# Decode attention and MLP on one core: the K and V tiles move from SyncE's DMA queue to GpSimd's software queue

## The chip, the cores and the metric

The kernel runs on one core of one Trainium2 chip. The metric is the device time of one execution in microseconds; for the kernel before it is 1303.65 us, the median of three runs (1303.53 to 1303.67). Profiles show one execution, from its first to its last instruction (the span). PE is TensorE, DVE VectorE, ACT ScalarE, POOL GpSimd and SP SyncE; SPq and POOLq are the sequencers of those two engines as they issue DMAs.

## The reference

One token for each of two sequences goes through an attention block with a cache of 8192 keys and values in 32 heads, then through a channel MLP. All is float32.

```python
# x (2,1,512)  k_cache, v_cache (2,32,8192,128)  wq (512,4096)  wo (4096,512)  w1 (512,1792)  w2 (1792,512)
q = (layernorm(x) @ wq).reshape(B, 1, 32, 128).transpose(0, 2, 1, 3)
p = softmax(einsum("bhqd,bhkd->bhqk", q, k_cache) * 128 ** -0.5)
o = einsum("bhqk,bhkd->bhqd", p, v_cache).transpose(0, 2, 1, 3).reshape(B, 1, 4096)
h = x + o @ wo
# the MLP block has a layernorm of its own, behind the outer one
out = h + gelu(layernorm(layernorm(h)) @ w1 + b1) @ w2 + b2
```

The two caches are 537 MB of the 561 MB that the kernel reads; each element of them is used once.

## The kernel before

The work is cut into 32 units. A unit is a pair of heads of one sequence: `units = [(g, b) ...]`, with g from 0 to 15 and b from 0 to 1, so even units have b = 0 and odd units b = 1. A unit has a K tile and a V tile, each of 128 partitions by 16384 float32 (64 KB a partition, 8 MB in all). All large tiles share a ring of three slots (`slot()`, the tile `kv`): wq takes the first, then K0, K1, V0, K2, V1, K3, V2 and so on, and a load waits until what stood in its slot has been read.

For each unit, `multiply` (L464, VectorE) multiplies a quarter of the K tile, a chunk of 32 keys a partition, by q in place. `halve` (L468, GpSimd) adds the upper 64 products of each key to the lower 64, for the first three chunks of the four. `add_up` (L471, VectorE) sums what is left to the scores. The loop over chunks c issues multiply(c), halve(c) and then add_up(c - 1), and add_up(3) comes after the loop. `row_max` (L478) and, at odd units, `all_max` and `exps` make the softmax weights of a pair (TensorE, VectorE, ScalarE). `values` (TensorE, L241 in the loop over rounds) multiplies the weights with a V tile: that of an even unit at the end of the odd unit after it, that of an odd unit at c == 2 of the even unit after it. So V(i - 2) has been read by the time that unit i is well under way, and K(i) by the end of unit i. At five places `stage` (L418) copies the next three pairs' q on VectorE, at c == 1 of odd units.

All loads of K and V come from one helper, `load` (L438), that issues on SyncE's hardware queue; `load_wo` (L444) loads most of wo into a slot and gathers the rest with two indirect DMAs on GpSimd (L448); `load_last` (L456) loads the tile `wlast`. SyncE does nothing else, so a load that waits for its slot holds up only the loads behind it. In the unit loop the loads of a unit are issued ahead of its computation, in this order: wo (last unit only), V(i - 1), K(i + 1), wlast (unit 30 only). After the loop come the last V tile in four parts, the bias, w1 and w2 (L667 to L675), on SyncE.

Engines take their instructions in program order. Semaphores and waits are put in by the class `Waits`, from what each instruction reads and writes; DMAs signal on 12 semaphores in turn, with separate sets for SyncE or ScalarE and for GpSimd. The program is built with `dynamic_dma_scratch_size=1024`, the space for descriptors of the software queue.

Of the kernel before, what the change touches and what calls it, by code (L numbers as in the profile page):

```python
# [22 lines left out]
GH = 3  # L23
SR = 4
LW = 4
LEFT = (((0, 3), (5, 19), (20, 30), (44, 47), (55, 56), (64, 66), (68, 94), (103, 105), (108, 109), (119, 121)),
        ((0, 2), (5, 11), (12, 30), (44, 47), (56, 57), (64, 66), (68, 95), (103, 104), (108, 109), (112, 113),
         (119, 121)))
# [2 lines left out]
def kept(left):  # L31
    at, runs, n = 0, [], 0
    for a, b in (*left, (P, P)):
        if a > at:
            runs.append((at, n, a - at))
            n += a - at
        at = b
    return runs, n
# [234 lines left out]
def tile_decode_block(nc, waits, x, k, v, wq, wo, wog, wol, w1, bias, w2, out):  # L273
    B, H, SK, DH = k.shape
    D = wq.shape[0]
    F = w1.shape[1]
    DC = D // P
# [3 lines left out]
    NS2 = SK // HP  # L281
    ROW = NS2 * DH
# [3 lines left out]
    NU = len(units)  # L286
# [10 lines left out]
    def slot():  # L297
        return kv.tile([P, ROW], F32, name="kv", tag="kv")
# [3 lines left out]
    junk = const.tile([P, 3], F32, name="junk")  # L302
# [1 line left out]
    x2 = const.tile([B, D], F32, name="x2")  # L304
    nc.scalar.dma_start(x2, x)
    wqt = slot()
    nc.sync.dma_start(wqt, wq.rearrange("(p r) n -> p (r n)", r=DC))
    wqs = wqt.rearrange("p (r n) -> p r n", r=DC)

    wlast = wts.tile([P, LW, D], F32, name="wlast")  # L310
    ident = const.tile([P, P], F32, name="ident")
# [7 lines left out]
    oall = const.tile([P, 2, 2 * GP, B], F32, name="oall")  # L319
    NQ = len(LEFT)  # L320
    og = const.tile([P, NQ * SR + LW - TH, B], F32, name="og")
    slots = [kept(x) for x in LEFT]
    first_slot = [sum(n for _, n in slots[:q]) for q in range(len(LEFT))]
    HG = H - LW
    NS = (HG - 4 * GP) * DH // SR
# [4 lines left out]
    pms = {}  # L330
    for x in LEFT:
        if x not in pms:
            pms[x] = const.tile([P, P], F32, name=f"pm{len(pms)}")
            nc.gpsimd.memset(pms[x], 0.0)
            for p0, s0, n in kept(x)[0]:
                nc.gpsimd.tensor_copy(pms[x][:, p0:p0 + n], ident[:, s0:s0 + n])
    pm = [pms[x] for x in LEFT]
    FAR = 4096.0
    ioff = const.tile([P, len(LEFT)], F32, name="ioff")
    for q in range(len(LEFT)):  # L340
# [89 lines left out]
    for _ in range(SPARE):  # L430
        pe.matmul(rowacc[:, :B], wz, wz, start=True, stop=True)

    def load(src, i, parts):
        g, b = units[i]
        t = slot()
        rows = src[b, 2 * g:2 * g + 2].rearrange("h (p j) d -> (h p) (j d)", j=NS2)
        for s0, n in parts:
            nc.sync.dma_start(t[:, s0 * DH:(s0 + n) * DH], rows[:, s0 * DH:(s0 + n) * DH])  # L438
        return t

    def load_wo():
        t = slot()
        n = 2 * GP * D
        nc.sync.dma_start(t[:, :2 * n], wo)  # L444
        tv = t[:, :2 * n].rearrange("p (j c) -> p j c", j=2)
        gv = t[:, 2 * n:].rearrange("p (q r n) -> p q r n", q=len(LEFT), n=D)
        for q in range(len(LEFT)):
            nc.gpsimd.indirect_dma_start(  # L448
                out=gv[:, q].rearrange("p r n -> p (r n)"), out_offset=None,
                in_=wog,  # L450
                in_offset=bass.IndirectOffsetOnAxis(ap=gidx[:, q:q + 1], axis=0),
                bounds_check=NS - 1, oob_is_err=False)
        return tv.rearrange("p j (r n) -> p j r n", n=D), gv

    def load_last():
        nc.sync.dma_start(wlast.rearrange("p r n -> p (r n)"), wol)  # L456

    def chunk(t, c):
        return t[:, c * CH * DH:(c + 1) * CH * DH].rearrange("p (j d) -> p j d", d=DH)

    def multiply(i, c, t):
        g, b = units[i]
        kc = chunk(t, c)
        nc.vector.tensor_tensor(kc, kc, QP[g][:, b, None, :].to_broadcast([P, CH, DH]), op=ALU.mult)  # L464

    def halve(c, t):
        kc = chunk(t, c)
        nc.gpsimd.tensor_tensor(kc[:, :, 0:HP], kc[:, :, 0:HP], kc[:, :, HP:DH], op=ALU.add)  # L468
# [36 lines left out]
    def inverse(g):  # L505
        r = work.tile(list(RL[g].shape), F32, name="rl" if g < GL else "rlp")
        nc.vector.reciprocal(r, RL[g])  # L507
        RL[g] = r

    def by_head(g):  # L510
        r = RL[g]
        RL[g] = work.tile([4, 2], F32, name="rl2")
        nc.vector.tensor_scalar(RL[g], hmask, r, None, op0=ALU.mult)
# [23 lines left out]
    def head_out(g):  # L537
        op, rl = OP.pop(g), RL.pop(g)
        if g < GL:
            nc.vector.tensor_tensor(orow[:, g % GH], op[:, None, :].to_broadcast([4, 2, DH]),  # L540
                                    rl[:, :, None].to_broadcast([4, 2, DH]), op=ALU.mult)
            return
        nc.vector.tensor_tensor(otz[:, :, 0:32:16], *(x.rearrange("p (b s) -> p s b", b=B) for x in (op, rl)),
                                op=ALU.mult)

    def turn(j):
        rows = orow.rearrange("m k e d -> m (k e d)")
        if j < 4:
            TP[j] = psm.tile([HP, 2 * GP, 2 * B], F32, name="sm")
            rows = rows.rearrange("m (p r) -> m r p", r=2 * GP)  # L550
            for r in range(2 * GP):
                pe.transpose(TP[j][:, r, :], rows[:, r, :], ident[:4, :4])
            psm.turn("sm", 2)
            return
        TP[j] = psm.tile([P, NQ * SR + LW - TH, 2 * B], F32, name="sm")
        at, n = (HG - 4 * GP) * DH, LW - TH
        last = rows[:, at:at + n * DH].rearrange("m (p r) -> m r p", r=n)
        for r in range(n):
            pe.transpose(TP[j][:, NQ * SR + r, :], last[:, r, :], ident[:4, :4])
        rows = rows.rearrange("m (s r) -> m r s", r=SR)  # L560
        for q, (_, n) in enumerate(slots):
            s0 = first_slot[q]
            for r in range(SR):
                pe.transpose(TP[j][:n, q * SR + r, :], rows[:, r, s0:s0 + n], ident[:4, :4])
# [21 lines left out]
    def project_all(wot, wgt):  # L586
        so = so2[0]
        parts = [(oall[:, j, r, :], wot[:, j, r, :]) for j in range(2) for r in range(2 * GP)]
        parts += [(og[:, q * SR + r, :], wgt[:, q, r, :]) for q in range(NQ) for r in range(SR)]
        parts += [(og[:, NQ * SR + h, :], wlast[:, h, :]) for h in range(LW - TH)]  # L590
        n = len(parts)
# [6 lines left out]

    full = [(0, NS2)]
    assert NS2 == NCH * CH  # L600
    KT, VT = {0: load(k, 0, [(0, NS2 // 2), (NS2 // 2, NS2 // 2)])}, {}
    for i, (g, b) in enumerate(units):
        if i == NU - 1:
            wot, wgt = load_wo()
        if i >= 1:
            VT[i - 1] = load(v, i - 1, full)
        if i + 1 < NU:
            KT[i + 1] = load(k, i + 1, full)
        if i == NU - 2:
            load_last()  # L610
        kt = KT.pop(i)
        S[i] = work.tile([P, NS2], F32, name="s", bufs=3)
        for c in range(NCH):
            multiply(i, c, kt)
            if c < NCH - 1:
                halve(c, kt)
            if c == 0:
                if b == 0 and g >= 1:
                    inverse(g - 1)
                if b == 1 and g >= 1:  # L620
                    head_out(g - 1)
                elif b == 1:
                    nc.vector.memset(orow, 0.0)
                if i == NU - 1:
                    turn(4)
            elif c == 1:
                if b == 0 and g >= 1:
                    by_head(g - 1)
                if b == 0 and g % GH == 1:
                    turned(max(g // GH - 1, 0))  # L630
                if i == NU - 1:
                    turned(4)
                if b == 1 and g < GL:
                    make_q(g + 1)
                    if g % GH == GH - 1:
                        stage((g + 1) // GH)
            if c >= 1:
                add_up(i, c - 1, kt, HP)
            if c == 2 and b == 0 and i >= 1:
                values(i - 1, VT.pop(i - 1))  # L640
                gather(g - 1)
                head_sum(g - 1)
                if g == GL:
                    pe.end()
            if c == 2 and i == NU - 1:
                placed()
                project_all(wot, wgt)
        add_up(i, NCH - 1, kt, DH)
        if b == 0 and g % GH == 0 and g < GL:
            pe.round()  # L650
        row_max(i)
        if i == NU - 1:
            row_sum()
        if b == 1:
            all_max(g)
            exps(g)
            values(i - 1, VT.pop(i - 1))
            total(g)
            if g % GH == 0 and g < GL:
                turn(max(g // GH - 1, 0))  # L660

    vlast = load(v, NU - 1, [(0, NS2 // 2), (NS2 // 2, 32), (NS2 // 2 + 32, 24), (NS2 - 8, 8)])
    wt = slot()
    br = wt[:, 2 * DC * F:2 * DC * F + FN + P]
    b1r, b2r = br[:, :FN], br[:, FN:]
# [167 lines left out]
```

## Time and profile before

| | |
|---|---|
| device time, median of 3 | 1303.65 us |
| span of the profiled execution | 1302.4 us |
| bytes moved by DMA, mean rate | 561.20 MB, 431 GB/s |
| VectorE busy | 951.3 us (73%) |
| GpSimd busy | 442.5 us (34%) |
| TensorE matmul busy | 386.7 us (30%) |
| the 96 halvings on GpSimd | 433.4 us |
| packets of the hardware queue q1 | 11114 |
| packets of the software queue q0 | 288 |

The page lists no device time for the profiled execution beside its span; the median of the runs lies 1.25 us above that span. The page's first part gives busy time by engine, its second cuts the span into 40 slices with a digit for the busy tenths, its third lists the DMA queues (q0 is GpSimd's software queue, q1 SyncE's hardware queue, q8 and q14 fetch instructions), the fourth follows the chain of work that ended last back from the end, and the fifth groups instructions: busy time and mean, then the idle time of the engine before them and what ended it. The timeline shows start, duration, engine, line, operation and tiles in order of time.

### The profile page before, as it was taken

The numbers are of one execution on the slowest core, as the hardware profiler recorded it, in microseconds if no ns is written. First come the engines' busy times: TensorE is split into PE (matmuls) and PEld (weight loads), VectorE is DVE, ScalarE is ACT, GpSimd is POOL, SyncE is SP. The second block draws the span as 40 slices with busy tenths as digits, with TensorE's granted clock in tenths as the row PEclk, the third lists the DMA queues.
The fourth block names the chain that finished last, engine by engine and source line by source line (L and its number), as shares of the span: only waits on it lengthen the run. The fifth ranks groups of instructions, "written<-read, shape, count | busy, mean of one in ns | idle before, by whom it ended". The sixth has DMA issues, their size and how long they took to land.

```text
span 1302.4 us, 6774 instructions
## 1 busy us (share of the span) xinstructions
PE 386.7 (30%) x2900; PEld 122.8 (9%) x2900; DVE 951.3 (73%) x411; ACT 51.7 (4%) x172; POOL 442.5 (34%) x138
## 2 busy tenths in 40 slices
PE   3105033330413314033230413323032331403358
PEld 1101000000100001010000101000010100100113
DVE  1988677779777778777778877777976777877752
ACT  0010000000000000000000000000000000000011
POOL 1444422244432234432234442224442224443320
PEclk9556566575666657566665666667566665756669
DMA  9999999999999999999999999999999999999998
GB/s 403 435 449 418 445 423 443 425 435 433 429 439 431 439 431 435 427 443 423 443 427 439 431 431 439 431 437 429 439 427 441 425 439 431 431 439 429 432 426 370
DMA packets 11420, 561.20 MB, mean 431 GB/s; under 512 B 1404, under 2 KB 1412, under 8 KB 1806
## 3 DMA queue, kind: packets, MB, share of 16 engines
q1 hardware_dynamic: 11114, 559.97, 99.5%
q0 software_dynamic: 288, 1.05, 0.2%
q8 instruction: 8, 0.13, 0.0%
q14 instruction: 6, 0.05, 0.0%
q10 hardware_dynamic: 4, 0.00, 0.0%
HBM read 562.06 MB, written 0.00 MB: 432 GB/s over the span
## 4 chain that ended last, share of the span: by engine, by line
DMA 46%; DVE 38%; PE 13%; ACT 1%; issue 1%; POOL 0%; SPq 0%; another core or an unknown queue 0%
DMA kv<-in_k_dram 41%; DVE kv L464 22%; DVE s L471 14%; PE so L241 11%; DMA kv<-in_w_dram 3%; DMA kv<-in_wq_dram 2%; PE sm L241 1%; ACT pt L495 1%; PE so L193 1%; DVE gm L483 0%; DVE mx L478 0%; DVE orow L540 0%; POOL kv L468 0%; DVE qs L418 0%; ACT nb L490 0%
## 5 line engine op out<-in xcount | busy, mean ns | idle before, releaser
L464 DVE TENSOR_TENSOR kv<-kv,qps 128x4096 f32<-128x4096 f32 x128 | 564.0, 4408 | 274.7 <-DMA kv<-in_k_dram 274.6
L468 POOL TENSOR_TENSOR kv<-kv 128x2048 f32<-128x2048 f32 x96 | 433.4, 4522 | 794.8 <-DVE kv L464 452.7
L471 DVE TENSOR_REDUCE s<-kv 128x32 f32<-128x2048 f32 (+1 forms) x128 | 357.2, 2810 | 0.7 <-POOL kv L468 0.3
L241 PE MATMUL so<-kv,pt 128*16 128x512 f32 x1920 | 277.7, 742 | 267.1 <-DMA kv<-in_v_dram 244.9
L241 PE MATMUL sm<-ident,mx 128*1 128x128 f32 x30 | 9.7, 325 | 568.1 <-DVE mx L478 568.1
L241 PEld LDWEIGHTS so<-kv,pt 128*16 128x16 f32 x1920 | 66.1, 113 | 453.9 <-DMA kv<-in_v_dram 246.3
L241 PEld LDWEIGHTS sm<-ident,mx 128*1 128x1 f32 x30 | 2.4, 79 | 574.2 <-DVE mx L478 571.1
L527 ACT ACTIVATE ss<-so 128x512 f32<-128x512 f32 x16 | 9.6, 597 | 553.7 <-PE so L241 516.1
L490 ACT ACTIVATE nb<-sm 128x4 f32<-128x4 f32 x16 | 2.8, 174 | 649.0 <-PE sm L241 646.9
L495 ACT ACTIVATE pt<-s,nb 64x128 f32<-64x128 f32 x64 | 25.5, 399 | 1.7
L193 PE MATMUL qps<-kv,pt 128*16 128x512 f32 x128 | 17.8, 690 | 8.6 <-DMA kv<-in_v_dram 8.6
L241 PE MATMUL sm<-ss,sel 128*4 128x128 f32 x120 | 15.6, 272 | 12.5 <-ACT ss L527 10.7
L404 DVE COPY q<-so 128x512 f32<-128x512 f32 x1 | 0.7, 690 | 19.5 <-PE so L193 19.5
L507 DVE RECIPROCAL rlp<-sm 128x4 f32<-128x4 f32 x1 | 0.2, 181 | 17.5 <-PE sm L193 17.5
L241 PEld LDWEIGHTS sm<-ss,sel 128*4 128x4 f32 x120 | 9.3, 87 | 28.2 <-ACT ss L527 17.3
L483 DVE TENSOR_REDUCE gm<-sm 1x4 f32<-1x256 f32 x16 | 6.6, 412 | 7.3 <-PE sm L241 7.0
L193 PE MATMUL so<-kv,yT 128*4 128x512 f32 x64 | 8.6, 700 | 11.2 <-DMA kv<-in_wq_dram 11.2
L495 ACT ACTIVATION_READ_ACCUMULATOR pt<-s,nb 64x1 f32 x64 | 11.8, 184 | 0.0
L241 PE MATMUL qps<-qs,pick 4*128 4x128 f32 x60 | 11.1, 306 | 0.0
L241 PE MATMUL sm<-gm,srow 1*128 1x4 f32 x30 | 8.7, 359 | 7.6 <-DVE gm L483 7.6
L478 DVE TENSOR_REDUCE mx<-s 128x1 f32<-128x128 f32 x32 | 9.1, 286 | 1.1
L193 PE MATMUL so<-kv,oall 128*2 128x512 f32 x48 | 7.6, 796 | 7.8 <-DMA kv<-in_wo_dram 7.8
(116 smaller groups left out, 130.7 us busy)
## 6 DMA issues: line engine op xcount, KB each, us to landing
kv<-in_k_dram SPq DMA_DIRECT2D x2, 4096.0 KB, 36.5
kv<-in_wo_dram SPq DMA_DIRECT2D x1, 6144.0 KB, 32.2
kv<-in_w_dram SPq DMA_DIRECT2D x3, 1792.0 KB, 34.5
kv<-in_v_dram SPq DMA_DIRECT2D x1, 4096.0 KB, 29.0
kv<-in_v_dram SPq DMA_DIRECT2D x1, 2048.0 KB, 27.3
kv<-in_v_dram SPq DMA_DIRECT2D x1, 1536.0 KB, 26.6
wlast<-in_wol_dram SPq DMA_DIRECT2D x1, 1024.0 KB, 37.1
kv<-in_w_dram SPq DMA_DIRECT2D x1, 1024.0 KB, 40.4
```

Source lines behind the costliest of these rows:

```text
L193: getattr(self.nc.tensor, what)(*aps, **how)
L241: ins = getattr(pe, what)(*aps, **how)
L404: nc.vector.tensor_copy(q2, so2[0])
L464: nc.vector.tensor_tensor(kc, kc, QP[g][:, b, None, :].to_broadcast([P, CH, DH]), op=ALU.mult)
L468: nc.gpsimd.tensor_tensor(kc[:, :, 0:HP], kc[:, :, 0:HP], kc[:, :, HP:DH], op=ALU.add)
L471: nc.vector.tensor_reduce(S[i][:, c * CH:(c + 1) * CH], chunk(t, c)[:, :, 0:n], axis=AX.X, op=ALU.add)
L478: nc.vector.tensor_reduce(MX[g][:, b:b + 1], S[i], axis=AX.X, op=ALU.max)
L483: nc.vector.tensor_reduce(gm, MT.pop(g).rearrange("o b (s p) -> o b s p", s=2), axis=AX.X, op=ALU.max, negate=True)
L490: nc.scalar.activation(nb, GM.pop(g), AF.Copy)
L495: nc.scalar.activation(ptz[b][q, :, 4 * m:4 * m + 4], s[q], AF.Exp, bias=nb[q, b, e:e + 1], scale=SCALE, accum_out=lt4[q, m:m + 1])
L507: nc.vector.reciprocal(r, RL[g])
L527: nc.scalar.activation(SS[g], so2[g == GL], AF.Copy)
```

## The change

K tiles, V tiles 0 to 30, the main part of wo and `wlast` are issued by GpSimd on the software queue, with `single_packet=True`: the eight rows that one DMA engine moves of a 128-row tile go as one packet. The last V tile, the bias, w1 and w2 stay on SyncE. wq is loaded in two parts, the first 14336 columns of a partition and the last 2048. A one-column copy on GpSimd that reads wq's first part stands ahead of the first K load, so that K0 is issued when that part has landed.

In the unit loop V(i - 1) is still issued at the unit's start, on GpSimd now, ahead of the unit's halvings. K(1) and K(2) are issued at the starts of units 0 and 1; from unit 2 to unit 30, K(i + 1) is issued at c == 2, behind the third halving in GpSimd's order, and `wlast` behind K31 in unit 30.

```diff
+QTAIL = 2048
...
-    nc.sync.dma_start(wqt, wq.rearrange("(p r) n -> p (r n)", r=DC))
+    wqv = wq.rearrange("(p r) n -> p (r n)", r=DC)
+    for a, e in ((0, ROW - QTAIL), (ROW - QTAIL, ROW)):
+        nc.sync.dma_start(wqt[:, a:e], wqv[:, a:e])
...
-    def load(src, i, parts):
+    def load(src, i, parts, soft=True):
...
-            nc.sync.dma_start(t[:, s0 * DH:(s0 + n) * DH], rows[:, s0 * DH:(s0 + n) * DH])
+            cols = slice(s0 * DH, (s0 + n) * DH)
+            if soft:
+                nc.gpsimd.dma_start(t[:, cols], rows[:, cols], single_packet=True)
+            else:
+                nc.sync.dma_start(t[:, cols], rows[:, cols])
...
-        nc.sync.dma_start(t[:, :2 * n], wo)
+        nc.gpsimd.dma_start(t[:, :2 * n], wo, single_packet=True)
...
-        nc.sync.dma_start(wlast.rearrange("p r n -> p (r n)"), wol)
+        nc.gpsimd.dma_start(wlast.rearrange("p r n -> p (r n)"), wol, single_packet=True)
...
+    nc.gpsimd.tensor_copy(junk[:, 0:1], wqt[:, 0:1])
     KT, VT = {0: load(k, 0, [(0, NS2 // 2), (NS2 // 2, NS2 // 2)])}, {}
     for i, (g, b) in enumerate(units):
         if i == NU - 1:
             wot, wgt = load_wo()
         if i >= 1:
             VT[i - 1] = load(v, i - 1, full)
-        if i + 1 < NU:
+        if i < 2:
             KT[i + 1] = load(k, i + 1, full)
-        if i == NU - 2:
-            load_last()
...
             multiply(i, c, kt)
             if c < NCH - 1:
                 halve(c, kt)
+            if c == 2 and 2 <= i < NU - 1:
+                KT[i + 1] = load(k, i + 1, full)
+            if c == 2 and i == NU - 2:
+                load_last()
...
-    vlast = load(v, NU - 1, [(0, NS2 // 2), (NS2 // 2, 32), (NS2 // 2 + 32, 24), (NS2 - 8, 8)])
+    vlast = load(v, NU - 1, [(0, NS2 // 2), (NS2 // 2, 32), (NS2 // 2 + 32, 24), (NS2 - 8, 8)], soft=False)
```

## The prediction

> **What bounds the kernel now.** I read the page first: the slices, the queues, the chain that ended last and the groups; then the rates by stage; then the timeline of one cycle of two units.
>
> ```profile
> span 1302.4 us, 6774 instructions
> ...
> DMA  9999999999999999999999999999999999999998
> ...
> q1 hardware_dynamic: 11114, 559.97, 99.5%
> q0 software_dynamic: 288, 1.05, 0.2%
> q8 instruction: 8, 0.13, 0.0%
> q14 instruction: 6, 0.05, 0.0%
> ...
> DMA 46%; DVE 38%; PE 13%; ACT 1%; issue 1%; POOL 0%; SPq 0%; another core or an unknown queue 0%
> ...
> L464 DVE TENSOR_TENSOR kv<-kv,qps 128x4096 f32<-128x4096 f32 x128 | 564.0, 4408 | 274.7 <-DMA kv<-in_k_dram 274.6
> L468 POOL TENSOR_TENSOR kv<-kv 128x2048 f32<-128x2048 f32 x96 | 433.4, 4522 | 794.8 <-DVE kv L464 452.7
> ```
>
> The DMA engines are busy in all 40 slices. VectorE's idle time before its multiplies, 274.6 us, is waiting for K. GpSimd waits for VectorE and is in no one's way. In three stretches of two cycles each (columns: window, length, engines, granted clock, DMA share, GB/s) the rate hardly moves:
>
> ```profile
> 605.00:682.50 77.50, 20.76 (x146) 5.97 (x146) 58.41 (x22) 2.73 (x10) 27.10 (x6) 0.63 1.01 436
> 682.50:760.00 77.50, 21.46 (x146) 6.06 (x146) 59.17 (x25) 2.73 (x10) 27.07 (x6) 0.63 1.00 434
> 760.00:837.00 77.00, 22.18 (x158) 8.51 (x158) 58.35 (x23) 2.73 (x10) 27.09 (x6) 0.61 1.00 432
> ```
>
> VectorE works 58.4 of 77.5 us there, so it could go faster; the DMA share of 1.00 could not. Now one cycle, unit 16 (the timeline: start, duration, engine, line):
>
> ```profile
> 605.12 4.42 DVE L464 TENSOR_TENSOR kv<-kv,qps 128x4096 f32<-128x4096 f32 x1 [9.40 <-DMA kv<-in_k_dram]
> ...
> 643.82 4.42 DVE L464 TENSOR_TENSOR kv<-kv,qps 128x4096 f32<-128x4096 f32 x1 [8.78 <-DMA kv<-in_k_dram]
> 645.87 0.33 SPq L438 DMA_DIRECT2D kv<-in_k_dram  x1
> ...
> 659.57 4.53 POOL L468 TENSOR_TENSOR kv<-kv 128x2048 f32<-128x2048 f32 x1 [2.25 <-DVE kv L464]
> 661.60 4.41 DVE L464 TENSOR_TENSOR kv<-kv,qps 128x4096 f32<-128x4096 f32 x1
> 663.18 9.25 PE L241 MATMUL so<-kv,pt 128*16 128x512 f32 x64 [17.45 <-DMA kv<-in_v_dram]
> ...
> 672.56 0.33 SPq L438 DMA_DIRECT2D kv<-in_v_dram  x1
> 672.93 0.43 SPq L438 DMA_DIRECT2D kv<-in_k_dram  x1
> 682.52 4.42 DVE L464 TENSOR_TENSOR kv<-kv,qps 128x4096 f32<-128x4096 f32 x1 [9.67 <-DMA kv<-in_k_dram]
> ```
>
> A K tile lands and the first multiply starts (643.82). The V tile behind it lands at 663.18, 19.36 us later: that is one 8 MB tile. The next K tile was queued at 645.87, 17 us before V was through, and lands for the multiply at 682.52. A cycle is 682.52 - 643.82 = 38.70 us, two tiles back to back, nothing else.
>
> **The change, part by part.** The steady part first, because it repeats. K(i+1) for i = 2 to 30, 29 tiles, is issued on GpSimd behind the third halving (L468 at c == 2) of unit i. That halving ends at 659.57 + 4.53 = 664.10, which is 20.28 us after the unit's first multiply and 0.92 us after V has landed. So the queue is empty when K is asked for, whatever the software queue costs. K's landing starts the next unit, and that unit's third halving asks for the next K: a loop that holds one K transfer and no V transfer. V(i) is issued at the next unit's start on GpSimd, behind K, when add_up has freed its slot (672.56 above, 8.5 us after K's issue): it still queues behind a K tile in flight and stays hidden. The new period is the time to the third halving's end, plus issue to use of a tile on idle engines.
>
> The first term is 20.28 us, and about 0.7 more in the five units that call stage (b = 1 of pairs 2, 5, 8, 11 and 14), where two L418 copies stand before the reduction:
>
> ```profile
> 691.62 0.71 DVE L418 TENSOR_REDUCE qs<-q 4x256 f32<-4x256 f32 x2
> ...
> 699.06 4.52 POOL L468 TENSOR_TENSOR kv<-kv 128x2048 f32<-128x2048 f32 x1 [2.88 <-DVE kv L464]
> ```
>
> Here 699.06 + 4.52 - 682.52 = 21.06. Over 29 units that averages 20.28 + 5 x 0.7 / 29 = 20.4.
>
> The second term has one row: wq, the same 8 MB, from SP onto idle engines (chain, start, duration), with the queue rows around it: no data before 1.70, three rows started by 1.80 (the window 1.2 to 1.8).
>
> ```profile
> 0.74 21.91 DMA kv<-in_wq_dram
> 22.70 8.77 PE so L193 x64
> ...
> 0.00:1.70 1.70, 0.00 (x0) 0.00 (x0) 0.79 (x6) 0.96 (x1) 1.09 (x7) 1.00 0.00 0
> ...
> DMA packets 3, 0.20 MB, mean 328 GB/s; under 512 B 0, under 2 KB 0, under 8 KB 0
> ```
>
> Issue to use is 22.70 - 0.74 = 21.96 us, and the first row moves about 1.0 us after issue. What the software queue adds has only the two gathers of wog as witness (the line's summary, the timeline, then the queues in the window 1215.6 to 1220.0 and in 1220 to 1221):
>
> ```profile
> L307 SPq DMA_DIRECT2D kv<-in_wq_dram x1: 397/397/397, 0.7 to 0.7; - x1
> ...
> L448 POOL DMA_INDIRECT kv<-in_wog_dram,gidx x2: 990/1114/1239, 1215.7 to 1217.2; - x2
> ...
> 1215.69 1.24 POOL L448 DMA_INDIRECT kv<-in_wog_dram,gidx  x1 [8.76 <-DVE s L471]
> 1217.23 0.99 POOL L448 DMA_INDIRECT kv<-in_wog_dram,gidx  x1 [0.30 <-issue]
> ...
> q1 hardware_dynamic: 29, 1.90, 99.7%
> ...
> q1 hardware_dynamic: 5, 0.33, 75.8%
> q0 software_dynamic: 4, 0.01, 2.2%
> ```
>
> An issue holds GpSimd 1.11 us against SP's 0.40, 0.7 more, and GpSimd took 0.30 to get to it. That makes 1.0 us extra, my value. The low end is nothing extra (SP's row as it is). The high end is the gathers' own start: none moved in the 4.3 us from 1215.69 to 1220.0, against 1.0 for SP, so 3.3 extra. Their engines were full of 64 KB rows, eight to a 19.36 us tile, so up to 2.4 of the 4.3 is a row in flight; I stay near the low end.
>
> Period: 20.4 + 1.0 + 21.96 = 43.36, against 38.70: 4.66 us more, 29 times, **135 us**. Ends: 42.36 gives 29 x 3.66 = 106; 45.66 gives 29 x 6.96 = 202.
>
> The Trainium skill, "DMA: Bandwidth & Descriptors", section Specifications, puts the first byte at about 1 us on the software path and 0.6 us on the hardware path. By that the extra would be 0.4, the period 42.76 and the sum 118 us. SP's first row at 1.0 us is nearer the page's other figure; no run here shows the software path on idle engines.
>
> Eight rows as one packet: I take nothing. The steady rows above show a DMA share of 1.00, so there is no gap to close; were the best window's rate (436) had everywhere in place of 434, a K tile would be 0.1 us shorter, 29 x 0.1 = 3 us less. Against it, 14 instruction packets would wait for a tile's packet instead of a row, up to 19.36 - 2.42 = 17 us each; none of the long waits of before is for code, and the queue now has pauses, so I leave it at nothing and in the upper end.
>
> The head: wq's second load is the last eighth, 2.4 us of its 19.36. GpSimd's new copy waits for the first seven eighths, at about 22.3 - 2.4 = 19.9, copies in 0.2, and K0's rows follow 2 us later, about when wq's tail is through: 0.3 us lost. Ends: 0, and about 4, if K0's packets get in ahead of wq's tail on some engines, which puts q, and all behind it, up to 9.7 us (half a tile) late, of which VectorE's idle time takes back more than half. V0 now comes behind unit 0's third halving, about 53, while K1 moves until about 61: hidden by K1.
>
> ```profile
> 1264.90 0.18 POOL L691 COPY kv<-ident 2x2 f32<-2x2 f32 x1
> ...
> 1225.37 4.42 DVE L464 TENSOR_TENSOR kv<-kv,qps 128x4096 f32<-128x4096 f32 x1 [9.67 <-DMA kv<-in_k_dram]
> ...
> 1299.12 1.18 PE qps L193 x24
> ```
>
> The tail, from the last unit's first multiply (1225.37) to the last weights (1299.12), is bytes in queue order: wlast, wo, V30, the last V, w1, w2. Those are all asked for before the queue is through, as now; SP's loads lose nothing by V30 being a packet, since they are behind it anyway. 0, at most some 4 us if code is late. The two gathers and V30 stand on GpSimd ahead of the last unit's halvings, which wait for K31 in any case.
>
> Sum: 1302.4 + 135 + 0.3 = 1437.7 us of span. Around the span of the profiled run lie 1.25 us to the median of 1303.65, so the forecast is **1439 us**.
>
> **The rivals.** *The other side:* GpSimd starts on K's descriptors when it takes up the third halving (659.57), not when that ends. The last V row is in about 0.5 us before 663.18, so the engines stay full if a software issue moves rows within 3.1 us; then K is hidden as now, and joined rows give at best 436 against 434 over 66 tiles, 6 us: 1297 to 1304, faster if any of it comes. Beyond 3.1 us it decides for slower again. For it: nothing but that GpSimd's next instruction needs no data of the halving. Against it: the second gather began 0.30 us after the first ended, one behind the other.
>
> *Descriptors wait for the multiply:* VectorE's running multiply keeps GpSimd from writing descriptors. The issue at 664.10 falls into the multiply 661.60 + 4.41 = 666.01, 1.9 us more: 29 x 6.56 = 190, 1494 us. Against it:
>
> ```profile
> L468 POOL TENSOR_TENSOR kv<-kv x96: 4508/4522/4532, 37.5 to 1241.3; 128x2048 f32<-128x2048 f32 x96
> ```
>
> All 96 halvings take the same time though many run beside a multiply, so a multiply does not shut GpSimd out. "SBUF — State Buffer", section SBUF: two separate sides, of the Trainium skill has this lock for VectorE's two-port modes; the trace bears it out little, since the halvings beside L464 are not stretched.
>
> *A slow software start:* 3.3 us extra every time: 202 + 1304 = 1506 us.
>
> *The change does nothing:* all queues end on the same 16 engines and K waits in line either way. It holds only if K is asked for before V is through, as in the first rival without the packets' gain: 1303.7 us.
>
> **How the numbers follow.** Longer loop with 0 to 2 us extra: 0.75, 1409 to 1468. Slow start 0.09, locked descriptors 0.07, faster 0.05, no change 0.03, other slower ways 0.01. Likeliest 1439. The range runs from 1403 (the low end, less packets' 3 us and a little) to 1500 (the locked descriptors with a margin); it leaves out the unchanged and faster cases and most of the slow start, under 2 in 10. A measurement of this kernel tells 0.2% from no change; slower takes 0.92, same 0.03, faster 0.05.
>
> **What would show it.** The DMA digits drop below 9 and the slices to about 434 x 38.70 / 43.36 = 387 GB/s; first multiplies stand 43.4 us apart; idle before L464 rises from 274.6 by about 135; POOL L468 enters the chain; each K issue on GpSimd starts within 0.5 us after a third halving and lands some 22.5 us later. Wrong, if K issues start with the halving, if the digits stay 9, or if issue to landing on idle engines is far from 22.5.

## The result, and the profile after

The changed kernel takes 1422.92 us (median of 4, 1422.52 to 1424.76) against 1303.59 us: a ratio of 1.0917, 95% interval 1.0901 to 1.0932. That is 119.3 us, or 9.2%, slower. The forecast was 1439 us. From the page of the profile after, the span, the slices, the two queues, the chain and three groups:

```profile
span 1422.7 us, 6773 instructions
...
GB/s 397 435 433 367 374 384 440 356 398 398 383 383 442 383 383 383 383 383 442 383 383 383 383 394 431 385 400 391 369 402 413 409 387 383 383 383 413 398 426 328
...
q0 software_dynamic: 9792, 536.88, 88.6%
q1 hardware_dynamic: 1754, 24.14, 4.0%
...
DMA 50%; DVE 36%; POOL 9%; PE 3%; another core or an unknown queue 1%; issue 0%; ACT 0%; DVEq 0%
...
L471 DVE TENSOR_TENSOR kv<-kv,qps 128x4096 f32<-128x4096 f32 x128 | 564.0, 4408 | 390.2 <-DMA kv<-in_k_dram 387.6
L475 POOL TENSOR_TENSOR kv<-kv 128x2048 f32<-128x2048 f32 x96 | 433.4, 4520 | 611.1 <-DVE kv L471 367.3
...
L443 POOL DMA_DIRECT2D kv<-in_k_dram x33 | 18.5, 562 | 8.3 <-DVE s L478 8.3
```

The lines are renumbered: L471 is the multiply, L475 the halving and L443 the load. Their busy times are those of before; what grew is VectorE's wait for K, from 274.6 to 387.6 us. The loss of transfer shows in the GB/s row of the slices: 383 in many of them, where the kernel before had 418 to 449 in all but the first and the last. GpSimd is now 9% of the chain, where it had 0%.

Where the 120.3 us of span went is seen by cutting both runs at the first multiply of unit 2 and of unit 31 (columns: window, length, busy time of PE, PEld, DVE, ACT and POOL with counts, granted clock, DMA share, GB/s). Before:

```profile
0.00:101.66 101.66, 22.14 (x241) 9.97 (x245) 63.81 (x44) 5.20 (x13) 32.46 (x42) 0.68 0.99 423
101.66:1225.37 1123.71, 317.84 (x2219) 97.47 (x2211) 850.38 (x335) 38.85 (x141) 394.97 (x89) 0.63 1.00 433
1225.37:1302.40 77.03, 46.73 (x444) 15.40 (x444) 37.10 (x34) 7.67 (x18) 15.03 (x7) 0.79 0.96 408
```

After:

```profile
0.00:102.48 102.48, 22.62 (x238) 10.83 (x242) 63.82 (x44) 5.20 (x13) 36.03 (x49) 0.67 0.99 421
102.48:1339.81 1237.33, 313.22 (x2223) 93.10 (x2215) 850.46 (x335) 38.86 (x141) 425.69 (x149) 0.62 0.92 393
1339.81:1422.70 82.89, 44.75 (x441) 15.55 (x444) 37.10 (x34) 7.67 (x18) 15.04 (x7) 0.74 0.91 389
```

Head +0.8, the 29 cycles +113.6, tail +5.9. A cycle is 1237.33 / 29 = 42.67 us, where it was 1123.71 / 29 = 38.75. One cycle of after, again of unit 16, from the timeline:

```profile
701.03 4.42 DVE L471 TENSOR_TENSOR kv<-kv,qps 128x4096 f32<-128x4096 f32 x1 [12.49 <-DMA kv<-in_k_dram]
...
716.79 4.52 POOL L475 TENSOR_TENSOR kv<-kv 128x2048 f32<-128x2048 f32 x1 [2.24 <-DVE kv L471]
718.82 4.41 DVE L471 TENSOR_TENSOR kv<-kv,qps 128x4096 f32<-128x4096 f32 x1
720.37 9.06 PE L242 MATMUL so<-kv,pt 128*16 128x512 f32 x64 [21.19 <-DMA kv<-in_v_dram]
721.25 0.56 POOL L443 DMA_DIRECT2D kv<-in_k_dram  x1
...
730.17 0.54 POOL L443 DMA_DIRECT2D kv<-in_v_dram  x1 [8.36 <-DVE mx L485]
743.44 4.42 DVE L471 TENSOR_TENSOR kv<-kv,qps 128x4096 f32<-128x4096 f32 x1 [13.36 <-DMA kv<-in_k_dram]
```

K is asked for the moment the third halving ends (721.25), 0.88 us after TensorE's first use of V (720.37), and is used 22.19 us after the request. V is asked for at 730.17 and hides behind it. Windows around the request show the engines standing still and then starting within a microsecond of each other:

```profile
721.25:722.40 1.15, 1.15 (x12) 0.28 (x8) 1.15 (x1) 0.00 (x0) 0.56 (x2) 0.50 0.00 0
722.40:723.20 0.80, 0.80 (x8) 0.17 (x4) 0.80 (x2) 0.00 (x0) 0.00 (x0) 0.50 3.77 1229
```

A packet (here a row of 64 KB) counts whole in the window in which it starts, hence a share over 1: 1229 GB/s over 0.80 us are 15 rows, so some 15 of the 16 engines begin K's first row between 722.40 and 723.20.

### The profile page after: what moved, and what is told of

The parts are those of the page before. It is cut to its first block, busy times and chain, and to the rows that moved or that the text cites. A ratio compares the mean times of both kernels' runs of the same rounds, so it can differ in the third digit from the quotient of the medians.

```text
span 1422.7 us, 6773 instructions
## 1 busy us (share of the span) xinstructions
PE 380.6 (27%) x2897; PEld 119.5 (8%) x2900; DVE 951.4 (67%) x411; ACT 51.7 (4%) x172; POOL 476.8 (34%) x205
## 4 chain that ended last, share of the span: by engine, by line
DMA 50%; DVE 36%; POOL 9%; PE 3%; another core or an unknown queue 1%; issue 0%; ACT 0%; DVEq 0%
DMA kv<-in_k_dram 48%; DVE kv L471 29%; POOL kv L475 9%; DVE s L478 6%; PE qps L194 2%; DMA kv<-in_wq_dram 1%; PE so L242 1%; DVE orow L547 0%; DVE rl L520 0%; PE sm L194 0%; PE so L194 0%; DVE qs L421 0%; ACT L502 0%; POOL kv L443 0%
## 5 line engine op out<-in xcount | busy, mean ns | idle before, releaser
L471 DVE TENSOR_TENSOR kv<-kv,qps 128x4096 f32<-128x4096 f32 x128 | 564.0, 4408 | 390.2 <-DMA kv<-in_k_dram 387.6
L475 POOL TENSOR_TENSOR kv<-kv 128x2048 f32<-128x2048 f32 x96 | 433.4, 4520 | 611.1 <-DVE kv L471 367.3
L242 PE MATMUL so<-kv,pt 128*16 128x512 f32 x1920 | 273.1, 732 | 326.2 <-DMA kv<-in_v_dram 304.0
L242 PEld LDWEIGHTS so<-kv,pt 128*16 128x16 f32 x1920 | 62.4, 112 | 512.0 <-DMA kv<-in_v_dram 305.5
L443 POOL DMA_DIRECT2D kv<-in_v_dram x31 | 16.6, 535 | 242.8 <-DVE mx L485 234.1
L194 PE MATMUL qps<-kv,pt 128*16 128x512 f32 x128 | 16.4, 663 | 18.6 <-DMA kv<-in_v_dram 18.6
L443 POOL DMA_DIRECT2D kv<-in_k_dram x33 | 18.5, 562 | 8.3 <-DVE s L478 8.3
L242 PEld LDWEIGHTS sm<-ss,sel 128*4 128x4 f32 x120 | 9.3, 87 | 28.2 <-ACT ss L534 17.2
L194 PE MATMUL so<-kv,yT 128*4 128x512 f32 x64 | 9.1, 736 | 9.5 <-DMA kv<-in_wq_dram 9.5
```

What stands on the lines that cost most here:

```text
L194: getattr(self.nc.tensor, what)(*aps, **how)
L242: ins = getattr(pe, what)(*aps, **how)
L443: nc.gpsimd.dma_start(t[:, cols], rows[:, cols], single_packet=True)
```

## The experiments

The theory was that the place of K's issue in GpSimd's order makes the loss, since K's transfer then starts only when the queue is empty. The main rival was that the software queue, or rows joined to a packet, is slow in itself.

**K behind the first halving.**

```diff
-            if c == 2 and 2 <= i < NU - 1:
+            if c == 0 and 2 <= i < NU - 1:
                 KT[i + 1] = load(k, i + 1, full)
```

> All as after, but K(i+1) is issued behind the first halving of unit i (c == 0) instead of the third. Theory (the loss is the place of the issue): the issue comes 9.1 us after the first multiply, V leaves the engines some 17 to 19 us after it, so the queue does not run empty and first multiplies stand 38.7 us apart again. Of the 119 us the 114 of the loop go and the head (0.8) and the tail (5.9) stay: 1310 us. Rival (the software queue or its joined rows are slow in themselves): above 1400 us. Third reading (joined rows are a gain that the loop hid): below 1304 us.

Measured: 1308.03 us (1306.86 to 1308.66), ratio to before 1.0030, interval 1.0021 to 1.0040. The three windows of this kernel:

```profile
0.00:103.43 103.43, 22.59 (x241) 10.96 (x245) 63.81 (x43) 5.20 (x13) 36.08 (x49) 0.67 1.00 425
103.43:1225.98 1122.55, 314.05 (x2219) 95.37 (x2211) 850.51 (x334) 38.85 (x141) 428.44 (x149) 0.63 1.00 433
1225.98:1306.40 80.42, 43.56 (x441) 15.44 (x444) 37.11 (x34) 7.67 (x18) 15.04 (x7) 0.75 0.91 389
```

On the same queue with the same packets the 29 cycles take 1122.55 us, a DMA share of 1.00 and 433 GB/s, as before. The whole loss of the loop was the place; the 4.3 us that are left lie in the head and the tail. Nothing is gained either: with `single_packet` the rows move on the software queue at the rate that they had on the other.

**K later still.** One more addition on GpSimd between the third halving and the load.

```diff
             if c == 2 and 2 <= i < NU - 1:
+                kc = chunk(kt, c)[:, :, HP:DH]
+                nc.gpsimd.tensor_tensor(kc, kc, kc, op=ALU.add)
                 KT[i + 1] = load(k, i + 1, full)
```

> All as after, with one more addition of 128x2048 on GpSimd (4.5 us, on products that nothing reads any more) between the third halving and K's issue. Theory (K's transfer hangs on GpSimd's order): each of the 29 cycles is 4.5 us longer, 42.7 to 47.2: 131 us more, 1554 us. Rival (the loss is a cost of each software issue, wherever it stands, or a lower rate of the transfers): within 10 us of 1423.

Measured: 1530.76 us, 107.8 more than after, not 131. The chain of this kernel shows why the number was off: this addition, both of whose inputs are the same data, costs 3.54 us on the path, not 4.5, and 29 x 3.6 = 104. The 29 cycles grew by 1343.55 - 1237.33 = 106.2 us, as their window shows above the chain; the rest is in the head and the tail.

```profile
102.31:1445.86 1343.55, 313.37 (x2215) 95.99 (x2207) 850.48 (x334) 38.85 (x141) 530.17 (x178) 0.61 0.85 362
...
628.33 4.53 POOL kv L475
632.93 3.54 POOL kv L625
636.47 22.17 DMA kv<-in_k_dram
```

All of GpSimd's added work appears in every cycle, and issue to use stays 22.2 us. The rival, within 10 us of 1423, falls.

**The place alone, on SyncE.** The kernel before, with K's issue (and that of wlast) moved behind the third halving and a wait of SyncE for GpSimd put there:

```diff
-        if i + 1 < NU:
+        if i < 2:
             KT[i + 1] = load(k, i + 1, full)
...
+            if c == 2 and 2 <= i < NU - 1:
+                nc.sync.wait_ge(waits.sems[("Pool",)], waits.count[("Pool",)])
+                KT[i + 1] = load(k, i + 1, full)
+            if c == 2 and i == NU - 2:
+                load_last()
```

> The kernel before, all loads on SyncE, but K(i+1) for i = 2 to 30 is issued only when the third halving of unit i has ended (SyncE waits for GpSimd there; wlast too). Theory (the place alone makes the loss): the cycle is 20.4 + 0.1 + 21.96 = 42.5 us, 29 x 3.75 = 109 us more, no loss in head or tail: 1412 us, and the software queue's own part of the loop is 29 x 0.2 = 6 us. Rival (the loss is the software queue's): 1304 us.

Measured: 1414.37 us, a ratio of 1.0847 (1.0825 to 1.0869). The middle and the last window of this kernel, K's transfer in its chain, and TensorE's first use of V30:

```profile
101.60:1333.91 1232.31, 314.12 (x2219) 95.01 (x2210) 850.40 (x334) 38.86 (x141) 395.02 (x89) 0.62 0.93 394
1333.91:1412.90 78.99, 45.82 (x441) 15.30 (x444) 37.11 (x34) 7.67 (x18) 15.02 (x7) 0.79 0.95 406
...
716.74 21.79 DMA kv<-in_k_dram
...
1373.28 8.75 PE L193 MATMUL qps<-kv,pt 128*16 128x512 f32 x64 [6.57 <-DMA kv<-in_v_dram]
```

The loop loses 1232.31 - 1123.71 = 108.6 us with no tile of K or V on the software queue. What that queue adds in the loop is 1237.33 - 1232.31 = 5.0 us, 0.17 a cycle. That is a difference of two things: on the mean of the 29 cycles SyncE, which waits for GpSimd first, asks for K 20.50 us after the unit's first multiply and GpSimd after 20.38; but from issue to use it is 21.99 us on SyncE's queue and 22.29 on the software queue, 0.30 more. The expectation of no loss in the tail missed: this kernel's tail is 1412.90 - 1333.91 = 79.0 us, 2.0 more than before, with the large loads still on one queue. The runs don't say why.

**Rows not joined.** `single_packet=True` is left out of all the loads.

> All as after, but the rows of an engine are not joined to one packet. Theory (rows move back to back either way, and a joined packet still takes turns with the hardware queue row by row): 1420 to 1426 us, the same tail. Rival (joined rows are worth what the best window's rate was over the mean, 6 us): 1429 us. Rival (a joined packet holds its engine): the tail changes by more than 5 us.

Measured: 1424.02 us (1423.66 and 1424.38), 1.1 us from after, and no tail of another length: 83.3 against 82.9 us. The queues in 20 us of the tail, when V30 (software queue, 64 KB rows) and the last V tile (SyncE's, 32 KB rows) are under way together, first in after (1363 to 1383), then without joining (1364 to 1384):

```profile
q0 software_dynamic: 91, 5.96, 69.0%
q1 hardware_dynamic: 84, 2.75, 31.9%
```

```profile
q0 software_dynamic: 89, 5.83, 67.5%
q1 hardware_dynamic: 85, 2.79, 32.3%
```

In both, the shares are two to one, as the rows' sizes are. If eight rows of the software queue held an engine for each row of the other, it would be sixteen to one. Eight rows of each in turn would give two to one as well, so the shares alone don't decide; the starts and ends of the rows do. Put together so that each row starts where another ends, they make 16 strings, one for each engine. In these 20 us a row of one queue is followed by one of the other in 157 of 159 places in after, and in 158 of 158 without joining: the queues take turns row by row in both.

**The tail.** V30 in two parts, and SyncE holds the last V tile back until the first part has landed:

```diff
-            VT[i - 1] = load(v, i - 1, full)
+            VT[i - 1] = load(v, i - 1, full if i < NU - 1 else [(0, 96)])
+            if i == NU - 1:
+                own = ('soft', (waits.lane['soft'] - 1) % Waits.LANES)
+                held = waits.sems[own], waits.count[own] * 16
...
+                nc.gpsimd.dma_start(VT[i - 1][:, cols], rows[:, cols], single_packet=True)
...
+    nc.sync.wait_ge(*held)
     vlast = load(v, NU - 1, ...)
```

> All as after, but V30 is loaded in two parts (three quarters, one quarter) and SyncE issues the last V tile only when the first part has landed, so that V30's rows share the engines with the last V tile's rows for its last 5 us instead of 25 us. Theory (the tail loses 5.9 us because rows of the two queues take turns, which makes V30 and the softmax-weighted sum behind it 12 us late): of the 5.9 us some 5 come back, 1418 us, V30 is used some 40 us after the last unit's first multiply instead of 49.5. Rival (the tail's loss comes from slower transfers on the software queue): 1423 us.

Measured: 1421.96 us, only 1.0 less than after. TensorE's first use of V30 in after and here:

```profile
1389.31 9.10 PE L194 MATMUL qps<-kv,pt 128*16 128x512 f32 x64 [18.64 <-DMA kv<-in_v_dram]
```

```profile
1375.08 9.35 PE L194 MATMUL qps<-kv,pt 128*16 128x512 f32 x64 [4.14 <-DMA kv<-in_v_dram]
...
1413.81 4.93 PE L194 MATMUL qps<-kv 128*32 128x128 f32 x112 [2.00 <-DMA kv<-in_w_dram]
```

The last unit begins at 1339.81 and at 1340.08, so V30 is used 49.5 us into it in after, and its first three quarters 35.0 us into it here: the taking of turns made it late, as the theory had it. But the tail shortens by only 2.1 us, to 1420.9 - 1340.08 = 80.8. Its end now waits for the last weights again (2.00 us before L194's last group): the loads that SyncE held back came late. In this profile the loop is 0.9 us shorter and the head 1.1 us longer than in after's; the eight kernels here with the same head have heads of 102.1 to 103.6 us, so about 1 us in a single profile is no effect.

**Both together, and wq in one load.** K early and the tail of the last experiment; then the same with wq whole:

```diff
-    for a, e in ((0, ROW - QTAIL), (ROW - QTAIL, ROW)):
+    for a, e in ((0, ROW),):
```

> e1 (K behind the first halving) with the tail of e5. Theory: the 3.4 us that e1's tail is longer than before go for the most part, the head's loss stays (1 to 2 us): 1305 us, the same as before within 0.2%. Rival (the software queue, once K is early and the tail in order, is worth something): below 1302 us.

> e6 with wq in one load, so that K0 is issued behind all of wq. Theory (the split lets K0's software start run beside wq's last eighth): K0 starts 2.3 us later and nothing behind takes it back: 2.3 us over e6, 1307 us. Rival (the head is hidden by the first unit's work): as e6.

Measured: 1305.17 us (ratio 1.0011, 1.0002 to 1.0021) and 1307.26 us (1.0029, 1.0017 to 1.0040). The first's windows:

```profile
0.00:102.39 102.39, 22.11 (x241) 10.68 (x245) 63.80 (x44) 5.20 (x13) 36.09 (x49) 0.67 0.98 420
102.39:1226.15 1123.76, 316.45 (x2223) 94.52 (x2214) 850.45 (x334) 38.88 (x141) 429.02 (x150) 0.63 1.00 433
1226.15:1303.70 77.55, 48.57 (x441) 15.74 (x444) 37.11 (x34) 7.67 (x18) 15.05 (x7) 0.79 0.95 404
```

With K in time and the tail in order, the software queue costs 1.5 us in all; in these profiles 0.7 us of it lie in the head, which varies by more than that, and 0.5 in the tail. Against e1, where only the tail differs, the tail edit takes 1308.03 - 1305.17 = 2.9 us off, more than in after. On this queue, wq in two loads saves 2.1 us against one load, as expected. No version here beats the kernel before.

**Wq in two loads alone**, on SyncE in the kernel before: the same two lines of the change.

> The kernel before with only wq in two loads, 14336 and 2048 columns, both on SyncE. Theory: TensorE starts on wq 2 us earlier, but the DMA engines move the same bytes in the same order and bound everything behind: 1303.7 us, the same. Rival (the head is on the path through q): 2 us less, 1301.7 us.

Measured: 1303.73 us, ratio 0.9999 (0.9990 to 1.0008). No difference. The split helped only where K0 is issued on another queue and waits for wq's first part.

**The threshold.** K behind the second halving; and behind the second halving with the same extra addition:

```diff
-            if c == 2 and 2 <= i < NU - 1:
+            if c == 1 and 2 <= i < NU - 1:
+                kc = chunk(kt, c)[:, :, HP:DH]
+                nc.gpsimd.tensor_tensor(kc, kc, kc, op=ALU.add)
                 KT[i + 1] = load(k, i + 1, full)
```

> All as after, but K(i+1) is issued behind the second halving (c == 1), 13.7 us after the unit's first multiply. Theory (what counts is whether K's rows stand at every engine when V's last row leaves it, 16.9 to 18.9 us after the first multiply; a software issue took 1.5 to 3.7 us to reach the first and the last engine in e7's trace, so by 17.4): as e1, 1308 us, first multiplies 38.7 us apart, at most 0.5 us more a cycle (15 us) if the slowest engine runs dry. Rival (a slower term in steps with the number of halvings ahead): half way between e1 and after, 1360 us.

> All as after, but K(i+1) is issued behind the second halving and one more addition of 3.6 us on products that nothing reads any more. The issue comes 13.66 + 0.07 + 3.60 = 17.3 us after the first multiply. Theory (the cycle is the larger of 38.70 and issue time + 22.2): 39.5 us, 29 x 0.83 = 24 us over e1: 1332 us. Rival (the loss comes from K's issue as such behind more than one halving, or in steps): 1308 or near 1423 us.

Measured: 1307.71 us without the addition (ratio 1.0031, 1.0019 to 1.0043), the same as behind the first halving, and 1366.62 us with it. So an issue 13.6 us into the unit is in time, and one 17.2 us into it is not. But the loss past the threshold was twice the forecast: 58.6 us over e1 instead of 24. K's transfers in four cycles of the chain, with the addition:

```profile
608.44 23.66 DMA kv<-in_k_dram
649.42 22.26 DMA kv<-in_k_dram
688.83 24.50 DMA kv<-in_k_dram
730.63 25.04 DMA kv<-in_k_dram
```

Over the 29 cycles, issue to use is 22.05 to 25.11 us, 23.52 on the mean, where it was 22.29 in after with the queue long empty. The rows, put together by engine as above, show what the long cycles wait for: one late engine. Where issue to use is at most 22.7 us, the last engine to resume after a pause begins K's rows within 2.6 us of the request; where it is over 24 us, 3.1 to 4.8 us after it. In every cycle that engine's eighth row ends 0.2 to 2.0 us before K is used, in the long ones 0.2 to 0.4. In the cycle of 730.63 the first engine begins 1.27 us after the request, the last but one 2.12 and the last 4.21, and V's last row on the engines that paused had ended by 0.76. So a request that comes as the engines run out pays the start anew, and at times one engine that is late by some 2 us more. Why that engine starts late, the runs don't say.

## Why the prediction was right, step by step

*What bounds it, and the loop.* Right. The prediction read from one cycle that K's request would come 0.92 us after V had landed; it came 0.88 after. It said that the loop would hold one K transfer and no V transfer, and the cycle of after is 20.22 (701.03 to 721.25) plus 22.19. SyncE with the same order loses 108.6 of the 113.6 us, near the prediction's low end of 106 for nothing extra. On the mean of the 29 cycles the request comes at 20.38 us (20.4 in the prediction), and on SyncE's queue issue to use is 21.99 us (21.96 there). A tile alone moves in 19.36 us, so of the 3.9 us that a cycle lost some 1.0 is the request's lateness and 2.9 the new start of engines that stood still.

*The size of the software issue.* Mis-sized: the term "1.0 us extra" a cycle measured 0.30 (22.29 against 21.99 us from issue to use). Neither of its two parts had the size it was given. The gathers' 1.11 us stood for a plain load's issue, which takes 0.56, 0.23 more than SyncE's 0.33; and the 0.30 us that GpSimd took between two gathers does not arise behind a halving, where the load starts as the halving ends. This is 29 x 0.7 = 20 of the 21.4 us by which the loop's 135 was too high. The high end took the 4.3 us without a software row for the gathers' own start. A plain load's first row moves 1.26 us after its issue on idle engines (mean of 29 cycles), so the 4.3 us were no measure of that; how much of them was a row in flight and how much the gather's own, no run separates.

The Trainium skill, "DMA: Bandwidth & Descriptors", section Specifications, gave 0.4 us for the software path over the other, an estimate of 118 us in all. That was nearer than the gathers: this case's traces show 0.30 us on the mean, and 113.6 us in the loop.

*The sum.* The nearness of 1439 to 1423 is in part luck. Of span, the loop came out 21.4 us under its term, the head 0.5 over and the tail 5.9 over: 15.0 us in all.

*Rows as one packet.* Right in taking nothing for it, as e1 and e4 show. No run shows that the option joins the rows at all. But the text also treated V30 as one packet that the last V tile would queue behind, and that is the step which failed in the tail: "SP's loads lose nothing by V30 being a packet, since they are behind it anyway". They were behind it while both stood in one queue. On two queues their rows take turns, V30 is used 49.5 us into the last unit instead of 37.3 (1262.71 in the profile before), and the tail is 5.9 us longer. Not all of that is the turns: with all large loads on SyncE and K late, the tail is already 2.0 us longer and V30 is used 39.4 us into the unit (1373.28 - 1333.91 in e3). Holding the last V tile back took 1.0 us off the device time in e5 and 2.9 in e6.

From the profile before:

```profile
1262.71 9.86 PE L193 MATMUL qps<-kv,pt 128*16 128x512 f32 x64 [6.47 <-DMA kv<-in_v_dram]
```

The same page of the Trainium skill, section "Queues, rings and completion order", has an engine drain a whole packet before it turns to another queue. Turns row by row, with and without `single_packet`, do not fit eight 64 KB rows as one packet that is drained whole; whether the rows were not joined or a packet does not hold the engine, the runs can't tell. That page of the Trainium skill, section "Issuing engines are not separate DMA queues", has all issuers interleave on the same 16 engines, and here the trace agrees (69.0% and 31.9%).

*The head.* 0.8 us against 0.3, within its bounds, but kernels with the same head have 0.4 to 1.9; with wq whole the device time is 2.1 us more.

*The rivals.* That GpSimd makes descriptors while the halving runs falls: K's issue stands at 721.25, the halving's end. That a running multiply locks GpSimd out falls too: K is issued at 721.25 and some 15 of its first rows begin at 722.40 to 723.20, all while the multiply 718.82 to 723.23 runs (its second input, q, lies in PSUM; other forms were not tried). A slow software start of 3.3 us falls with the 0.30 measured, and a change without effect with the result.

## What to carry to other kernels

When a queue is full all the time, the order of the issues is part of the schedule: a load may be issued late only as long as its rows reach the engines before the rows ahead of it run out. Here V was used some 19.4 us into the unit, a request for K at 13.6 us was in time and one at 17.2 was not; the limit lies between. Before a load is moved onto an engine that also computes, find the instruction that it will stand behind, and compare that one's end with the landing of the transfer ahead in the queue. Loads that were in order on one queue are in order no longer when they are split over two; what must land first has to be kept on the same queue or held back by a wait.

## What the runs showed of the hardware that was not expected

A plain load in the loop holds GpSimd for 0.53 to 0.60 us, half of an indirect one (0.99 to 1.24), and its first row moves 1.26 us after its start on idle engines, where SyncE's moves after 0.96 (means of 29 cycles in after and e3). A standstill of the engines costs more than that start: in after the 16 engines resume over 0.84 us, and the first row of each takes 3.1 us where the later ones take 2.42, so that issue to use is 22.29 us for a tile whose eight rows an engine take 19.36. Two queues share an engine row by row, 69.0% to 31.9% for rows of 64 and 32 KB, and `single_packet` did not change it. An addition of 128x2048 elements takes GpSimd 3.60 us when both inputs are the same data, and 4.52 in the halving, where they are not. Past the threshold the loss sets in faster than the lateness: a request 0.8 us too late by a plain sum (17.2 + 22.29 - 38.7) cost 2.0 us a cycle (58.6 / 29).
